# The first batch of a retention and mixer kernel: state sums, query scaling and constants in another order, and two weight loads moved

## The chip, the cores and the metric

The kernel runs on one core of a Trainium2 chip. The metric is the device time of one execution in microseconds (us). TensorE (PE) multiplies matrices, VectorE (DVE), ScalarE (ACT) and GpSimd (POOL) work elementwise, and SyncE (SP) and GpSimd start transfers between memory and the core.

## The reference

Inputs are q, k and v of 8 batches, 8 heads, 576 positions and 64 dimensions, and the weights U (576 x 32), V (32 x 576), w_ch1 (512 x 2048) and w_ch2 (2048 x 512), all in 32-bit floats.

```python
scores = (q @ k.transpose(0, 1, 3, 2)) / 8
gamma  = 1.0 - 2.0 ** (-5.0 - arange(8))            # one decay per head
rel    = pos[:, None] - pos[None, :]
x      = (scores * where(rel >= 0, gamma ** rel, 0)) @ v   # heads side by side: (8, 576, 512)
u      = x + (x.transpose(0, 2, 1) @ U @ V).transpose(0, 2, 1)
out    = u + maximum(u @ w_ch1, 0.0) @ w_ch2
```

The decay factors into one power of the query's position and one of the key's, so it is put into scaled queries or outputs, and into scaled keys.

## The kernel before

**Pairs and chunks.** Batches are worked in four pairs. The 1152 rows of a pair are nine chunks of 128; the middle one, J, holds the last 64 rows of one batch and the first 64 of the next. Batches after the first pair are cast, transposed by transfers and multiplied chunk by chunk in `section`.

**The first pair** is handled apart, since at the start everything waits for memory. Its rows are four units of 256 (u = 0 to 3 in the code, units one to four in the text), two for each batch, and the middle chunk J, in two halves. Lines are those of the kernel before:

- `early_consts` (L117) builds position and decay tables, masks and zeroed buffers on GpSimd, VectorE and ScalarE.
- `load_u` and `load_J` issue the loads of q, k and v on SyncE's queue. `load_w1` (L212) and `load_w2` issue the weights on GpSimd's queue, in pieces; `load_w1(f0, f1)` brings the columns of the groups f0 to f1 - 1.
- `scale_u` (L637) scales a unit's keys by `vscaleU` to bf16, `cast_u` (L630) casts queries and values, `cast_J` (L799) makes J's keys and queries; J's queries in the first half are scaled by `posJ` (L805).
- `T_u` (L646) transposes keys or queries on TensorE and copies them out. `SC_u` (L675) computes the scores of half of the heads, `mask_u` (L690) multiplies them with a triangle on VectorE (L692). `SC_off` (L719) computes the scores between the two rows of unit one and copies them to a buffer `off`. `RV_u` and `RV_off` multiply scores with values.
- `ST_u` (L760) sums key-value products of a unit into an accumulator, and `Sblk` (L770) copies that as a state block into `sblk`. `QS_u` (L744) adds queries times state to a unit's outputs. `XS_u` (L752) brings the outputs to the buffer `x`, on VectorE, times `qscale`.
- `T_J`, `SC_J`, `mask_J`, `RV_J`, `QS_J` and `XS_J` do the same for J.
- `warm(n)` (L205) issues n multiplications of the identity whose result is not used.
- `to_xT` transposes x, `MA` is the product with U, and then `first_stretch` (L1033) runs the products with w_ch1 (L515), group by group of 128 columns (f = 0 to 15), between the steps of units three and four. Its `y(n)` issues the next n groups. A piece of w1 has to be there when its first group comes.
- After unit four a one-element write by VectorE (L1089) releases the eight loads of w2.

**What sets the order.** The whole program is inside `tc.manual_schedule()`: every engine takes its instructions in the order in which the code issues them. Within one engine nothing overtakes. Buffers come from pools: PSUM has one buffer each of `psc` (`ps_sc`), `po` (`ps_o`) and `pss` (`ps_s`), and three of `big`. The next user of a buffer waits until its last reader is done. `SC_u(0, 1)` and then `SC_off(1)` both take `ps_o`, and `RV_u(0, ...)` takes `ps_sc` after `SC_u(1, 0)`.

## Time and profile before

| | us |
|---|---|
| median of 4 runs | 325.98 |
| lowest and highest of them | 325.44, 326.66 |
| the profiled execution | 327.3 |
| its span, from first to last instruction | 325.5 |
| TensorE busy | 311.1 |
| VectorE busy | 174.3 |
| ScalarE busy | 145.8 |
| GpSimd busy | 101.2 |

Times in the profile are counted from the start of the span. In the views of groups and of time, a line tells start or busy time, engine, code line, operation, what it writes and reads, and in brackets the idle time ahead of it with what ended that idle time. TensorE is the engine with the most work; idle time of the others costs nothing by itself. "Landing" of a transfer is the moment at which its last part is in place.

### The profile page before, as it was taken

The page shows a single profiled execution, that of the slowest core. Times are in us where ns is not written, and L with a number is a line of the kernel's source. Part 1 is how long each engine was busy: PE and PEld are TensorE (multiplying, and loading weights), DVE is VectorE, ACT ScalarE, POOL GpSimd, SP SyncE. Part 2 cuts the span into 40 slices and gives each one's busy share as a digit, 9 for nine tenths or more (in the row PEclk, how much of TensorE's full clock was granted, in tenths as well). Part 3 has the DMA queues.
Part 4 walks back from the last instruction along what each step waited for, and adds up shares of the span by engine and source line. Part 5 has one row for each costly group of instructions (what it writes and reads, how often), then busy time and mean ns, then how long its engine had stood idle before and what let it go on. Part 6 is the DMA issues. An engine that isn't in the chain of part 4 may idle for free.

```text
span 325.5 us, 9118 instructions
## 1 busy us (share of the span) xinstructions
PE 311.1 (96%) x3860; PEld 170.9 (53%) x3885; DVE 174.3 (54%) x342; ACT 145.8 (45%) x334; POOL 101.2 (31%) x172
## 2 busy tenths in 40 slices
PE   7899889999999999989999999999999999999996
PEld 3575545764444454446744454457644454467544
DVE  7866556229726578545844477556844475510012
ACT  6857547892020583048810484058800572047400
POOL 7796239223113722052221523152221500010000
PEclk9999999999999999999999999999999999999999
DMA  8999999999975989969996599859996450340022
GB/s 216 253 217 262 239 201 193 203 179 119 255 185 138 243 179 176 218 156 193 192 174 171 143 186 206 214 144 167 208 207 158 107 67 3 102 110 0 2 76 85
DMA packets 152904, 53.30 MB, mean 164 GB/s; under 512 B 132032, under 2 KB 150336, under 8 KB 152864
## 3 DMA queue, kind: packets, MB, share of 16 engines
q1 hardware_dynamic: 144512, 40.40, 67.8%
q0 software_dynamic: 8352, 12.32, 15.5%
q8 instruction: 30, 0.49, 0.6%
q14 instruction: 10, 0.08, 0.1%
HBM read 36.85 MB, written 9.44 MB: 142 GB/s over the span
## 4 chain that ended last, share of the span: by engine, by line
PE 72%; DMA 6%; ACT 3%; DVE 2%; issue 1%; DVEq 0%; SPq 0%
PE ps_y L549 34%; PE ps_y L515 30%; DMA qkT<-qk 5%; PE pp L296 2%; DVE u L464 2%; DMA uT<-u 1%; ACT y L520 1%; PE pp L316 1%; PE ps_y L560 1%; PE pp L328 1%; PE AB L358 1%; PE pa L431 1%; PE ph L458 1%; ACT s_sb L373 1%; ACT uT L489 0%
## 5 line engine op out<-in xcount | busy, mean ns | idle before, releaser
L515 PE MATMUL ps_y<-uT,w_sb 128*128 128x256 bf16 (+2 forms) x768 | 133.3, 326 | 2.6 <-DMA uT<-u 1.0
L520 ACT ACTIVATE y<-ps_y 128x384 bf16<-128x384 f32 (+2 forms) x192 | 89.6, 490 | 97.8 <-PE ps_y L515 97.0
L549 PE MATMUL ps_y<-w_sb,y 128*128 128x512 bf16 x535 | 123.8, 379 | 2.2 <-issue 1.1
L515 PEld LDWEIGHTS <-w_sb 128*128 128x128 bf16 x768 | 72.1, 98 | 50.6 <-issue 3.6
L549 PEld LDWEIGHTS <-y 128*128 128x128 bf16 x560 | 52.5, 98 | 61.2
L272 POOL TENSOR_TENSOR vt<-stage_t,vscale 64x256 bf16<-64x256 f32 (+1 forms) x81 | 50.4, 622 | 65.1 <-DMA stage_t<-in_v_dram 49.2
L538 DVE TENSOR_TENSOR o_sb<-ps_y,u 128x512 f32<-128x512 f32 (+2 forms) x38 | 25.2, 664 | 81.3 <-PE ps_y L549 79.0
L541 POOL DMA_DIRECT2D out_dram<-o_sb x31 | 17.1, 553 | 104.1 <-DVE o_sb L538 100.3
L304 DVE TENSOR_TENSOR ret<-pp,triH 128x512 bf16<-128x512 f32 x27 | 18.7, 691 | 24.5 <-PE pp L328 17.9
L464 DVE TENSOR_TENSOR u<-ph,xt 128x768 bf16<-128x768 f32 (+2 forms) x24 | 21.8, 950 | 5.9 <-PE ph L458 4.2
L437 ACT ACTIVATE a_sb<-pa 128x128 bf16<-128x128 f32 x8 | 2.2, 277 | 43.9 <-PE pa L431 43.9
L338 DVE COPY q<-qkT 64x256 bf16<-64x256 bf16 x48 | 14.1, 293 | 14.1 <-DMA qkT<-qk 13.2
L344 DVE TENSOR_TENSOR xt<-pp,qscale 128x512 bf16<-128x512 f32 x27 | 18.6, 689 | 4.7 <-PE pp L328 4.2
L263 DVE CAST qk<-stage_t 64x256 bf16<-64x256 f32 x54 | 19.2, 356 | 1.3
L383 DVE TENSOR_TENSOR s_sb<-AB,Af 64x256 bf16<-64x256 f32 x42 | 17.7, 422 | 2.1 <-ACT s_sb L378 1.5
L264 ACT ACTIVATE qk<-stage_t 128x512 bf16<-128x512 f32 x27 | 16.8, 622 | 0.0
L635 POOL CAST qk<-stage_t 128x512 bf16<-128x512 f32 x16 | 10.2, 638 | 11.6 <-DMA stage_t<-in_q_dram 6.5
L376 ACT ACTIVATE Af<-AB 128x256 f32<-128x256 f32 x24 | 9.2, 385 | 8.2 <-PE AB L358 7.7
L692 DVE TENSOR_TENSOR ret<-psc,triU 128x1024 bf16<-128x1024 f32 x8 | 9.6, 1206 | 3.3 <-PE psc L684 3.3
L261 ACT ACTIVATE qk<-stage_t 128x256 bf16<-128x256 f32 x27 | 11.1, 410 | 0.0
L296 PEld LDWEIGHTS <-qkT 64*64 64x64 bf16 x432 | 5.6, 107 | 10.2 <-issue 7.8
L209 PE MATMUL pw<-ident 128*128 128x512 bf16 x26 | 8.0, 452 | 1.4 <-POOL ident masks.py:199 1.4
(134 smaller groups left out, 220.0 us busy)
## 6 DMA issues: line engine op xcount, KB each, us to landing
stage_t<-in_k_dram SPq DMA_DIRECT2D x32, 256.0 KB, 4.8
stage_t<-in_q_dram SPq DMA_DIRECT2D x32, 256.0 KB, 5.5
stage_t<-in_v_dram SPq DMA_DIRECT2D x32, 256.0 KB, 5.7
out_dram<-o_sb POOLq DMA_DIRECT2D x31, 256.0 KB, 3.2
w_sb<-in_moe_w_ch_dram POOLq DMA_DIRECT2D x14, 256.0 KB, 8.1
stage_t<-in_k_dram SPq DMA_DIRECT2D x8, 128.0 KB, 3.3
stage_t<-in_q_dram SPq DMA_DIRECT2D x8, 128.0 KB, 3.6
stage_t<-in_v_dram SPq DMA_DIRECT2D x8, 128.0 KB, 4.1
```

Of the source, the lines that this page charges most:

```text
L263: nc.vector.tensor_copy(out=o[to, hl], in_=f[fr, hl])
L264: nc.scalar.activation(out=c["qk"][:, 0, :], in_=c["f", 0].rearrange("p h d -> p (h d)"), func=AF.Copy)
L272: nc.gpsimd.tensor_tensor(out=o[to, hl], in0=f[fr, hl], in1=w[fr, hl, :, None].to_broadcast([n, NHP, D]), op=ALU.mult)
L304: nc.vector.tensor_tensor(out=ret.rearrange("p a b i -> p a (b i)").rearrange("p a (b i) -> p a b i", i=D), in0=pp[:, :, 0:NHP * D].rearra ...
L344: nc.vector.tensor_tensor(out=st["x", pr][:, i, :].rearrange("p (hp hl d) -> p hl hp d", hl=2, d=D), in0=pp[:, :, NHP * D:2 * NHP * D].rea ...
L383: nc.vector.tensor_tensor(out=S_[half(x), 1, :], in0=Bk[half(1 - x)], in1=Af[half(1 - x), now, :], op=ALU.add)
L464: nc.vector.tensor_tensor(out=st["u", par][:, i0 - base:i0 - base + n, w].rearrange("p s (c d) -> p c s d", c=2), in0=ph[k][:, :, 0:n, :], ...
L515: nc.tensor.matmul(ps[:, 0:n, :], w1_sb[:, cc, f * P:(f + 1) * P], st["uT", par][:, c0:c0 + n, cc, :], start=(cc == 0), stop=(cc == NCC - 1),)
L520: nc.scalar.activation(out=st["y1", par][:, f, c0 * P:(c0 + n) * P], in_=ps[:, 0:n, :].rearrange("p s t -> p (s t)"), func=AF.Relu)
L538: nc.vector.tensor_tensor(out=o_sb[:, 0:n], in0=ps[:, 0:n], in1=st["u", par][:, c, w], op=ALU.add)
L541: (nc.sync if last else nc.gpsimd).dma_start(out=out_flat[r0:r0 + P, w], in_=o_sb[:, 0:n])
L549: nc.tensor.matmul(ps, st["y1", par][:, f, c * P:(c + 1) * P], w2_sb[:, f, :], start=(f == 0), stop=(f == NF - 1),)
```

## The change

It is made in `early_consts` and `startup`, and in three helpers that they call:

- In `early_consts`, ScalarE computes an exponential of `posU` for unit one. The position table, `qscale` and `vscale` are made ahead of the triangle `triU`. The zeroing of `sblk` and of `off` on VectorE moves here from `startup`.
- Unit one's queries are multiplied with that table on GpSimd instead of being cast, and `XS_u(0)` becomes a copy on ScalarE instead of a product on VectorE.
- `cast_J(0)` takes GpSimd for the keys instead of ScalarE, keeps VectorE for the queries, and stands ahead of unit two's transposes instead of behind its first mask. The first piece of w1 is issued right after it.
- Three warm-up multiplications after `SC_off(1)` go. Both sums of unit one (`acc1`, `acc2`) and the first state block come in their place. `T_J(0)` comes before unit one's outputs, and the sums and state blocks of unit two before its outputs.
- The steps from `RV_u(1, 1)` to `XS_J(0)` are written ahead of the casts and loads of GpSimd, with which they share no engine's order.
- `load_w1(10, 14)` moves from ahead of the keys and queries of unit four to behind them.

```diff
@@ -150,27 +150,31 @@
             out=posU.rearrange("p u j h -> p (u j) h"),
             in0=lngt[:, 0:8, :], in1=posU.rearrange("p u j h -> p (u j) h"), op=ALU.mult)
         nc.scalar.activation(out=vscaleU, in_=posU, func=AF.Exp, bias=lnb, scale=-1.0)
+        nc.scalar.activation(
+            out=posU[:, 0], in_=posU[:, 0], func=AF.Exp, bias=0.0, scale=1.0)
         nc.vector.tensor_scalar(
             out=posJ, in0=posJ, scalar1=0.5, scalar2=None, op0=ALU.mult)
         nc.vector.tensor_tensor(out=posJ, in0=posJ, in1=lngt[:, 0:2, :], op=ALU.mult)
         nc.scalar.activation(out=vscaleJ, in_=posJ, func=AF.Exp, bias=lnb, scale=-1.0)
         nc.scalar.activation(out=posJ, in_=posJ, func=AF.Exp, bias=0.0, scale=1.0)
+        nc.vector.tensor_scalar_add(pos[:, J + 1:NI, :], pos[:, J + 1:NI, :], -float(S))
+        nc.vector.tensor_scalar_add(pos[HALF:P, J, :], pos[HALF:P, J, :], -float(S))
+        nc.vector.tensor_tensor(out=lngt, in0=lngt, in1=pos, op=ALU.mult)
+        nc.scalar.activation(out=qscale, in_=lngt, func=AF.Exp, bias=0.0, scale=1.0)
+        nc.scalar.activation(out=vscale, in_=lngt, func=AF.Exp, bias=lnb, scale=-1.0)
         nc.vector.tensor_scalar(
             out=triU[0:HALF], in0=iotaU[0:HALF], scalar1=0.0, scalar2=None, op0=ALU.is_ge)
         nc.vector.tensor_scalar(
             out=triU[HALF:P], in0=iotaU[HALF:P], scalar1=-float(P), scalar2=None,
             op0=ALU.is_ge)
-        nc.vector.tensor_scalar_add(pos[:, J + 1:NI, :], pos[:, J + 1:NI, :], -float(S))
-        nc.vector.tensor_scalar_add(pos[HALF:P, J, :], pos[HALF:P, J, :], -float(S))
-        nc.vector.tensor_tensor(out=lngt, in0=lngt, in1=pos, op=ALU.mult)
-        nc.scalar.activation(out=qscale, in_=lngt, func=AF.Exp, bias=0.0, scale=1.0)
-        nc.scalar.activation(out=vscale, in_=lngt, func=AF.Exp, bias=lnb, scale=-1.0)
-        nc.vector.tensor_copy(out=triH[0:HALF], in_=tri[0:HALF, 0:HALF])
-        nc.vector.tensor_copy(out=triH[HALF:P], in_=tri[HALF:P, HALF:P])
+        nc.vector.memset(sblk, 0.0)
+        nc.vector.memset(un[0]["off"][HI], 0.0)
         nc.vector.memset(U_E[:, J, :], 0.0)
         nc.vector.memset(U_O[0:HALF, 0, :], 0.0)
         nc.vector.memset(V4[:, 0:HALF], 0.0)
         nc.vector.memset(V4[:, HALF + S:], 0.0)
+        nc.vector.tensor_copy(out=triH[0:HALF], in_=tri[0:HALF, 0:HALF])
+        nc.vector.tensor_copy(out=triH[HALF:P], in_=tri[HALF:P, HALF:P])
         nc.vector.tensor_copy(out=swap[:, 0:HALF], in_=ident[:, HALF:P])
         nc.vector.tensor_copy(out=swap[:, HALF:P], in_=ident[:, 0:HALF])
 
@@ -634,11 +638,11 @@
         else:
             eng.tensor_copy(out=o, in_=f)
 
-    def scale_u(u, hh, eng):
-        o, f = unit_views(u, 1, hh)
+    def scale_u(u, hh, eng, j=1):
+        o, f = unit_views(u, j, hh)
         eng.tensor_tensor(
             out=o, in0=f,
-            in1=vscaleU[:, u, :, 4 * hh:4 * hh + 4].rearrange("p j h -> p h j")[
+            in1=(posU, vscaleU)[j][:, u, :, 4 * hh:4 * hh + 4].rearrange("p j h -> p h j")[
                 :, :, :, None].to_broadcast([P, 4, 2, D]),
             op=ALU.mult,
         )
@@ -751,6 +755,11 @@
 
     def XS_u(u, c0=0, c1=2):
         i0, n = unit_i0(u) + c0, c1 - c0
+        if u == 0:
+
+            nc.scalar.activation(
+                out=st["x", 0][:, 0:2, :], in_=un[0]["po"], func=AF.Copy)
+            return
         nc.vector.tensor_tensor(
             out=st["x", 0][:, i0:i0 + n, :].rearrange("p s (h d) -> p s h d", d=D),
             in0=un[u]["po"][:, c0:c1, :].rearrange("p s (h d) -> p s h d", d=D),
@@ -904,7 +913,10 @@
         for hh in range(2):
             scale_u(u, hh, nc.gpsimd)
         for hh in range(2):
-            cast_u(u, 0, hh, nc.gpsimd)
+            if u == 0:
+                scale_u(u, hh, nc.gpsimd, 0)
+            else:
+                cast_u(u, 0, hh, nc.gpsimd)
 
     def startup():
         load_u(0, (1, 0))
@@ -921,7 +933,6 @@
         warm(10)
         cast_unit(0)
         T_u(0, 1, nc.vector)
-        nc.vector.memset(un[0]["off"][HI], 0.0)
         zero_J(1, nc.vector)
         load_J(1, (1, 0, 2))
         load_u(2, (1, 0, 2))
@@ -935,8 +946,9 @@
         cast_unit(1)
         cast_u(0, 2, 0, nc.gpsimd)
         cast_u(0, 2, 1, nc.gpsimd)
+        cast_J(0, nc.gpsimd, nc.vector)
+        load_w1(0, 2)
         cast_u(1, 2, 0, nc.gpsimd)
-        load_w1(0, 2)
         cast_u(1, 2, 1, nc.gpsimd)
         T_u(1, 1, nc.scalar)
         SC_u(0, 1, ps_o, "po")
@@ -944,32 +956,38 @@
         SC_off(0, ps_sc, "psc")
         warm(3)
         T_u(1, 0)
-        nc.vector.memset(sblk, 0.0)
         SC_off(1, ps_o, "po")
-        warm(3)
+        acc1 = pss_tile()
+        acc2 = ps_big.tile([P, NHP, P], FP32, tag="big", name="pss2")
+        ST_u(0, ALL, acc1, True)
+        Sblk(acc1, 1)
+        ST_u(0, ALL, acc2, True)
         SC_u(1, 0, ps_sc, "psc")
         mask_u(1, 0)
-        cast_J(0, nc.scalar, nc.vector)
         SC_u(1, 1, ps_o, "po")
         mask_u(1, 1)
-
-        acc1 = pss_tile()
-        ST_u(0, ALL, acc1, True)
-        Sblk(acc1, 1)
+        T_J(0)
         RV_u(0, 0)
         RV_u(0, 1)
         RV_off()
         XS_u(0)
-        T_J(0)
-        acc2 = ps_big.tile([P, NHP, P], FP32, tag="big", name="pss2")
-        ST_u(0, ALL, acc2, True)
+        SC_J(0)
+        mask_J(0)
         prep_vJ(0)
         cast_urows()
-        RV_u(1, 0)
-        SC_J(0)
-        mask_J(0)
         ST_u(1, LO, acc1, False)
         Sblk(acc1, 2)
+        ST_u(1, ALL, acc2, False)
+        Sblk(acc2, 3)
+        RV_u(1, 0)
+        RV_u(1, 1)
+        QS_u(1, 0, 1)
+        XS_u(1, 0, 1)
+        QS_u(1, 1, 2)
+        XS_u(1, 1, 2)
+        RV_J(0)
+        QS_J(3)
+        XS_J(0)
         cast_J(1, nc.gpsimd, nc.gpsimd)
         load_w1(2, 4)
         prep_vJ(1)
@@ -982,23 +1000,13 @@
         load_w1(8, 10)
         for hh in range(2):
             cast_u(2, 2, hh, nc.gpsimd)
-        load_w1(10, 14)
         scale_u(3, 0, nc.gpsimd)
         for hh in range(2):
             cast_u(3, 0, hh, nc.gpsimd)
+        load_w1(10, 14)
         load_w1(14, 16)
         for hh in range(2):
             cast_u(3, 2, hh, nc.gpsimd)
-        RV_u(1, 1)
-        QS_u(1, 0, 1)
-        XS_u(1, 0, 1)
-        ST_u(1, ALL, acc2, False)
-        Sblk(acc2, 3)
-        QS_u(1, 1, 2)
-        XS_u(1, 1, 2)
-        RV_J(0)
-        QS_J(3)
-        XS_J(0)
 
         xT = [ps_big.tile([P, dm], FP32, tag="big", name="xT") for _ in range(3)]
         xT.append(ps_sc.tile([P, dm], FP32, tag="psc", name="xT"))
```

## The prediction

> **What bounds the kernel now.** I read the page's busy table first, then its 40 slices, then TensorE's timeline with the waits in brackets.

> ```profile
> PE 311.1 (96%) x3860; PEld 170.9 (53%) x3885; DVE 174.3 (54%) x342; ACT 145.8 (45%) x334; POOL 101.2 (31%) x172
> ...
> PEclk9999999999999999999999999999999999999999
> ```

> TensorE is busy 311.1 of 325.5 us at full clock. The change touches only the first 48 us, so its worth is what it adds to or takes from TensorE's work and idle time there, as far as later waits do not swallow it. The table of stages gives TensorE 7.84, 8.94, 9.12, 9.09 and 9.13 us busy in the first five tens, 19.47 of 20 from 80 to 100 and 170.19 of 175 after 150: idle time worth having is all early. In TensorE's timeline of 0 to 48 us these lines matter:

> ```profile
> 11.65 0.41 PE L726 MATMUL psx<-qkT 64*64 64x128 bf16 x8 [0.35 <-DVE ret L692]
> 11.99 0.82 PE L209 MATMUL pw<-ident 128*128 128x512 bf16 x3
> 12.65 0.61 PE L655 MATMUL pst<-ident,qk 128*128 128x128 bf16 x8
> 13.19 0.41 PE L726 MATMUL psx<-qkT 64*64 64x128 bf16 x8
> 13.54 0.82 PE L209 MATMUL pw<-ident 128*128 128x512 bf16 x3
> 14.29 0.86 PE L684 MATMUL psc<-qkT 64*64 64x128 bf16 x32
> ...
> 16.21 0.64 PE L711 MATMUL po<-qk,ret 64*128 64x64 bf16 x32 [0.52 <-DVE ret L692]
> ...
> 38.42 0.51 PE L655 MATMUL pst<-ident,qk 128*128 128x128 bf16 x6 [0.91 <-POOL qk L635]
> ...
> 41.91 0.38 PE L763 MATMUL pss<-qk 64*128 64x128 bf16 x4 [0.42 <-POOL qk L635]
> 42.23 0.42 PE L684 MATMUL psc<-qkT 64*64 64x128 bf16 x16
> 42.58 1.04 PE L515 MATMUL ps_y<-uT,w_sb 128*128 128x512 bf16 x4
> ```

> Start, duration, group, then idle time and its releaser. Up to 24 us TensorE idles in short pieces; the second batch of cross scores (L726, 13.19) waits for nothing. At 38.42 and 41.91 it waits for GpSimd's casts of unit four's queries and values, which come from memory. At 42.58 stands the eleventh group of the first matrix (f = 10).

> VectorE's timeline, SyncE's, and the transfer view cut to the moment of one issue:

> ```profile
> 10.44 2.29 DVE L692 TENSOR_TENSOR ret<-psc,triU 128x1024 bf16<-128x1024 f32 x2
> 13.30 0.73 DVE L665 COPY qkT<-pst 128x512 bf16<-128x512 bf16 x1 [0.57 <-PE pst L655]
> ...
> 16.08 0.85 DVE L805 TENSOR_TENSOR qk<-stage_t,posJ 128x512 bf16<-128x512 f32 x1
> ```
> ```profile
> 9.04 0.82 SPq L796 DMA_DIRECT2D stage_t<-in_q_dram  x1
> ```
> ```profile
> stage_t<-in_q_dram SPq DMA_DIRECT2D x1, 128.0 KB, 5.0
> ```

> The queries of the middle chunk J are issued at 9.04 and land 5.0 us later, at **14.0**. Before, VectorE scales them (L805) at 16.08, long after, and both of unit one's masks are over at 12.73.

> [...] GpSimd's in-order queue sits 1.42 us before the value cast at 14.90, and the w1 issue behind it comes only at 15.46. [...] This trace has no gap over 1.4 us and a granted clock of 1.0 throughout[...]. [...] with w1 in flight from 36.8 to 40.5 us the DMA share is 1.19, and SyncE's last loads take 7 to 12 us instead of 5.

> **The change part by part.**

> *Queries of unit one scaled instead of cast.* Two GpSimd casts (0.63 and 0.61, L635) become two products with a scale, at 1.06 as L639. The first starts at 6.34 as before; the second ends at 8.46 instead of 7.78. TensorE's transposes at 7.84 start 0.65 later. ScalarE's added exponential (0.22, like L157) lies before 3.4 us, covered by the wait for the first keys. Unit one's output copy leaves VectorE (1.21, L754) for ScalarE (1.02, like L730).

> *Constants reordered.* VectorE clears sblk and the cross buffer (0.91 each) ahead of the key copy L669, which then ends near 9.4 instead of 7.60. The second small product of L199 needs its PSUM buffer and TensorE gets there near 9.2: +0.2. The earlier qscale and vscale have no early reader: zero.

> *J's query cast moved ahead of the mask of unit one's second half.* The instruction order of the changed kernel shows VectorE: first mask, J's scaling (waiting for that transfer), second mask. Nothing before it in SyncE's queue moves, so I keep 14.0. Scaling 14.05 to 14.90, mask 14.90 to 16.10 (1.15 to 1.21, L692). Behind it stand VectorE's copy of unit two's queries and the second cross scores, which need that PSUM buffer. They start at **16.15 instead of 13.19**. TensorE is ready near 14.1, so it idles 2 us; the +0.65 and +0.2 above vanish inside this.

> *From there to the transposition of x.* Before, 13.19 to 21.83, 8.64 us. After, by starts: cross scores 0.35 (16.50); both sums of unit one 1.12 in place of three warm-ups of 0.75 (17.62); scores of unit two 0.79 (18.41); J's transposes 0.44 (18.85). The outputs of unit one take the buffer that the first mask of unit two frees: scores out at 18.05, 0.15 to VectorE, 1.19 of mask, 19.40, so 0.55 idle, as 0.52 before. Outputs 1.06 (20.46), J's scores 0.2, the sums of unit two 1.05 (21.7), its outputs 0.75 (22.45). The second state product starts 1.18 after the first, as before (19.73, 20.91), since the copy-out of the first row of the same tile lies between; the sum that stood in this gap has moved away, so it is idle now. 23.63, then 0.92 as before: **24.55, +2.7**. The gains (0.75 of warm-ups, waits of 0.17 and 0.34) are spent on this gap and the sums' new place. ScalarE's outputs of unit one (20.6 to 21.7) push the later state copies to 23.2, before their reader at 24.2: free.

> *GpSimd's part of that.* J's key cast moves there (0.60, from ScalarE's 0.62) into a 1.42 wait and w1's first piece is issued 1.35 earlier; nothing on TensorE reads it before 27: zero, or a few tenths late for unit two's values, which have 2 us of slack.

> *w1 pieces behind unit four's queries.* Before:

> ```profile
> 30.56 0.74 POOL L214 DMA_DIRECT2D w_sb<-in_moe_w_ch_dram  x1
> ...
> 37.75 0.61 POOL L635 CAST qk<-stage_t 128x512 bf16<-128x512 f32 x1 [2.14 <-DMA stage_t<-in_q_dram]
> 38.30 0.81 POOL L214 DMA_DIRECT2D w_sb<-in_moe_w_ch_dram  x1
> ```
> ```profile
> w_sb<-in_moe_w_ch_dram POOLq DMA_DIRECT2D x1, 512.0 KB, 9.9
> ```

> The piece for f = 10 to 13 is issued at 30.56 and lands at 40.5, 2.1 us early. Now it stands behind the query casts. The software queue moved 0.45 MB in 34 to 38 us, much of it this piece, so the last queries may land up to 1 us sooner; the issue then falls at 37.5 to 38.4. A 256 KB piece takes 5.5 to 6.0 us from issue with nothing ahead of it (the ones at 15.46 and 38.30), a further 256 KB 1.8 to 3 more: landing 44.5 to 47; I take **45.2**, towards the early end[...]. TensorE comes to f = 10 at 42.58 + 2.7, less the two waits at 38.42 and 41.91 that a late TensorE no longer meets (0.91 + 0.42): 44.0. Stall 1.2 (0 to 3). The next piece has 4 us more.

> *Sum.* +2.7 − 1.3 + 1.2 = +2.6. The matrix loads of w2 start as much later; between 50 and 80 us the waits for transposes, uT and y come to 2 us, but casts, w2 and transposes hang on the same shifted TensorE, so I let them swallow 0.2 only. **+2.4 us.** Against the profiled execution (327.3, of which 325.5 span) that is 329.7; that execution lies 1.3 above the median 325.98, so the forecast is **328.4**.

> **The rivals.** *w1 in time.* If the piece lands by 44.0 only +1.4 is left, less 0.2: 327.2. For it: freed transfer time. Against: 5.5 us even for half its size.

> *Swallowed.* If in addition the waits of 50 to 80 us swallow half a microsecond or more, 326.5, no measurable change. For it: transposes that take 6.5 and 5.1 us there. Against: their casts shift with TensorE.

> *Faster.* J's queries land by 11.4, before the first mask's end less the scaling; then the second mask is not held and TensorE reaches unit four with no delay, where queries a microsecond sooner take away the waits of 0.91 and 0.42: about −1.0, 325.0. It decides at a landing of 11.4 against 14.0 seen; 2.6 us is far.

> *Worse.* The 2 us gap beside the shorter ones halves the granted clock for a window, or w1 lands at 47: +4.5, 330.5.

> The change's scheduling does reach the instruction streams, so "it does nothing" is no case.

> **How the numbers follow.** Forecast 0.52, w1 in time 0.26, swallowed 0.09, faster 0.05, worse 0.08. 0.3% of this kernel is 1.0 us, about what a measurement tells from no change; "faster" takes its case, "same" the swallowed one with the low edge of w1 in time (0.10), "slower" the rest (0.85). The likeliest case alone spans 327.5 to 330; the range reaches down through w1 in time and up to the worse case: 326.6 to 330.6.

> **What would show it.** In the changed profile: VectorE idle about 1.7 us before J's scaling, released by the transfer of q; the second cross scores of TensorE near 16.1, after about 2 us idle on VectorE's mask; the transposition of x near 24.5; no wait on GpSimd for unit four's queries; at f = 10 a wait for w1. I am wrong if J's scaling does not wait, if x is transposed before 23, or if w1's late piece is never waited for.

## The result, and the profile after

The changed kernel takes 327.95 us (median of 38 executions, 326.37 to 330.5) against 325.97 (57 executions, 324.56 to 330.63): **ratio 1.0064, 95% interval 1.005 to 1.0078**, 2.0 us slower. (That of the two medians is 1.0061; ratios below are the recorded ones too.) The forecast was 328.4, 2.4 us slower than 325.98. The profiled execution takes 327.94 us, of which 326.2 are its span.

The page of the changed kernel, busy times and granted clock:

```profile
PE 311.4 (95%) x3857; PEld 171.2 (52%) x3882; DVE 174.3 (53%) x341; ACT 146.3 (45%) x335; POOL 102.6 (31%) x173
...
PEclk9799999999999999999999999999999999999999
```

TensorE is busy as long as before. New is the second digit of the clock: 7 where before every slice had 9. The profiled execution is thus one of those in which the clock dropped; none of the changed kernel at full clock was profiled. TensorE's timeline of the changed kernel:

```profile
8.24 0.28 PE L659 MATMUL pst<-ident,qk 128*128 128x128 bf16 x2 [0.72 <-POOL qk L643]
9.25 0.51 PE L659 MATMUL pst<-ident,qk 128*128 128x128 bf16 x6 [0.73 <-POOL qk L643]
9.69 0.38 PE L203 MATMUL pv<-V_b,fan 32*128 32x512 bf16 x1
10.98 0.18 PE L203 MATMUL pv<-V_b,fan 32*128 32x64 bf16 x1 [0.90 <-DVE qkT L673]
11.10 2.29 PE L213 MATMUL pw<-ident 128*128 128x512 bf16 x5
13.32 0.64 PE L688 MATMUL psc<-qkT 64*64 64x128 bf16 x16
...
17.03 0.41 PE L730 MATMUL psx<-qkT 64*64 64x128 bf16 x8
...
24.24 0.40 PE L750 MATMUL po<-sblk,qkT 128*128 128x128 bf16 x4 [0.79 <-DVE xt L763]
...
25.16 0.62 PE L1017 MATMUL xT<-ident,xt 128*128 128x128 bf16 x8
...
40.57 0.61 PE L659 MATMUL pst<-ident,qk 128*128 128x128 bf16 x8
...
43.69 0.62 PE L772 MATMUL pss<-qk 64*128 64x128 bf16 x8
...
44.59 1.04 PE L519 MATMUL ps_y<-uT,w_sb 128*128 128x512 bf16 x4
```

The same steps in the kernel before:

```profile
7.84 0.51 PE L655 MATMUL pst<-ident,qk 128*128 128x128 bf16 x6 [0.24 <-POOL qk L635]
...
8.63 1.25 PE L209 MATMUL pw<-ident 128*128 128x512 bf16 x5
9.82 0.42 PE L684 MATMUL psc<-qkT 64*64 64x128 bf16 x16
...
21.83 0.62 PE L1009 MATMUL xT<-ident,xt 128*128 128x128 bf16 x8
```

Three readings. The first scores of unit one (L688) start at 13.32; before they started at 9.82. So 3.5 us are lost already here, ahead of the step where the prediction put its loss. From here on the gap hardly grows: x is transposed (L1017) at 25.16 instead of 21.83, +3.3. Then the waits for unit four's queries and values are gone (40.57 and 43.69 have no bracket, where 0.91 and 0.42 stood), and the eleventh group (44.59, f = 10) comes 2.0 us later than its 42.58, with no wait for w1. The end is 2.0 us later by the medians too. The two profiled spans differ by 0.7 only. In part that is because the waits of TensorE after 48 us hold one in the kernel before that the changed one lacks:

```profile
PE ps_y L515 <- DMA uT<-u: 1.0, 1, 1.0
```

The 3.5 us can be split in that view. The second transposes of unit one's queries begin at 9.25 instead of 7.84: +1.41. VectorE's copy holds the second product of L203, so that the warm-ups of L213 begin at 11.10 instead of 8.63: +1.06 more. Five warm-ups take 2.22 us to the next group instead of 1.19: +1.03. VectorE's and GpSimd's timelines of the changed kernel tell where the first two come from:

```profile
6.41 0.91 DVE L171 MEMSET y<- 64x1024 uint32 x1 [0.27 <-issue]
...
7.57 0.64 DVE L176 COPY triH<-y 64x64 bf16<-64x64 bf16 x1
8.22 1.00 DVE L177 COPY triH<-y 64x64 bf16<-64x64 bf16 x1
9.24 1.00 DVE L178 COPY swap<-ident 128x64 bf16<-128x64 bf16 x1
10.16 0.17 DVE L179 COPY swap<-ident 128x64 bf16<-128x64 bf16 x1
10.25 0.68 DVE L673 COPY qkT<-pst 128x1024 bf16<-128x1024 bf16 x1
...
14.01 1.23 DVE L696 TENSOR_TENSOR ret<-psc,triU 128x1024 bf16<-128x1024 f32 x1 [1.47 <-PE psc L688]
15.15 0.68 DVE L814 TENSOR_TENSOR qk<-stage_t,posJ 128x512 bf16<-128x512 f32 x1
15.75 1.22 DVE L696 TENSOR_TENSOR ret<-psc,triU 128x1024 bf16<-128x1024 f32 x1
```
```profile
7.12 2.07 POOL L643 TENSOR_TENSOR qk<-stage_t,posU 128x512 bf16<-128x512 f32 x2 [1.25 <-DMA stage_t<-in_q_dram]
9.15 2.09 POOL L643 TENSOR_TENSOR qk<-stage_t,vscaleU 128x512 bf16<-128x512 f32 x2
```

VectorE's copies in the kernel before:

```profile
4.84 1.03 DVE L168 COPY triH<-y 64x64 bf16<-64x64 bf16 x1
5.89 0.18 DVE L169 COPY triH<-y 64x64 bf16<-64x64 bf16 x1
...
6.32 0.18 DVE L174 COPY swap<-ident 128x64 bf16<-128x64 bf16 x1
6.42 0.59 DVE L175 COPY swap<-ident 128x64 bf16<-128x64 bf16 x1
6.92 0.68 DVE L669 COPY qkT<-pst 128x1024 bf16<-128x1024 bf16 x1
```

The query products start at 7.12, 0.78 after the cast of before (6.34), since the transfer came later in this execution, and take 2.07 instead of two casts. The clearings (that of L171, named `y`, is of the cross buffer `off`) end at 7.32, and now the small copies of the constants fall beside four GpSimd products in a row, which end about 8.16, 9.19, 10.2 and 11.2. The copies L176 to L178 end at 8.21, 9.22 and 10.24, each as a product ends; L179, of the same shape as L178, takes 0.17. Behind them the key copy (L673) ends at 10.93; before (L669) it ended at 7.60. In the kernel before two of the copies are long in the same way: L168 (1.03) ends at 5.87 and L175 (0.59) at 7.01, beside a product and a cast of GpSimd that end at 5.84 and 6.97; L169 and L174 take 0.18. What makes them end together was not shown.

J's scaling (L814) does not wait: no bracket. J's queries had landed at 14.53, and the mask ahead of it ended later because the first scores were late. TensorE hardly waits behind it either: its transposes end at 16.90, the second mask at 16.97, and the second cross scores start at 17.03.

### The profile page after: what moved, and what is told of

Read it like the earlier page. It is cut to its first block, busy times and chain, and to the rows that moved or that the text cites. A ratio compares the mean times of both kernels' runs of the same rounds, so it can differ in the third digit from the quotient of the medians.

```text
span 326.2 us, 9115 instructions
## 1 busy us (share of the span) xinstructions
PE 311.4 (95%) x3857; PEld 171.2 (52%) x3882; DVE 174.3 (53%) x341; ACT 146.3 (45%) x335; POOL 102.6 (31%) x173
## 4 chain that ended last, share of the span: by engine, by line
PE 74%; ACT 4%; DMA 3%; DVE 2%; issue 1%; DVEq 0%
PE ps_y L553 34%; PE ps_y L519 32%; PE pp L300 2%; DVE u L468 2%; DMA qkT<-qk 1%; ACT y L524 1%; DMA uT<-u 1%; PE pp L320 1%; PE pp L332 1%; PE ps_y L564 1%; PE AB L362 1%; PE pa L435 1%; PE ph L462 1%; ACT s_sb L377 1%; ACT qk L268 0%
## 5 line engine op out<-in xcount | busy, mean ns | idle before, releaser
L639 POOL CAST qk<-stage_t 128x512 bf16<-128x512 f32 x14 | 9.1, 671 | 4.1 <-DMA stage_t<-in_q_dram 3.6
L213 PE MATMUL pw<-ident 128*128 128x512 bf16 x23 | 8.1, 507 | 1.4 <-POOL ident masks.py:199 1.4
## 6 DMA issues: line engine op xcount, KB each, us to landing
stage_t<-in_k_dram SPq DMA_DIRECT2D x8, 128.0 KB, 3.7
stage_t<-in_q_dram SPq DMA_DIRECT2D x8, 128.0 KB, 4.0
stage_t<-in_v_dram SPq DMA_DIRECT2D x8, 128.0 KB, 3.8
```

## The experiments

Every ratio is to the kernel before, run in turn on the same chip. "Full" counts executions whose mean granted clock over the span is 0.998 or more, "low" the others; the median of each is shown as a ratio to the median of before. One window of 3.41 us at half clock brings that mean to 0.995 (as in u_zero's profile), and most low executions are at 0.994 or 0.995. The kernel before had medians of 325.97, 326.56, 326.59 and 327.26 in four series (after; u_zero to b_w1; u_scale to b_split in the table; the last four), so small differences between ratios of different series are less sure than the intervals say.

| kernel | ratio [95%] | full: number, ratio | low: number, ratio |
|---|---|---|---|
| after | 1.0064 [1.005, 1.0078] | 20, 1.0034 | 18, 1.0089 |
| u_zero | 1.0038 [1.0021, 1.0055] | 6, 1.0007 | 13, 1.0041 |
| u_jq | 1.0022 [1.0003, 1.004] | 11, 0.9984 | 11, 1.0047 |
| u_zero_jq | 0.9998 [0.9979, 1.0018] | 17, 0.9979 | 5, 1.0067 |
| b_w1 | 1.0017 [0.9995, 1.0039] | 12, 0.9978 | 10, 1.0055 |
| u_scale | 1.0058 [1.0039, 1.0078] | 9, 1.0043 | 13, 1.0072 |
| clk | 1.0041 [1.002, 1.0062] | 9, 1.0036 | 4, 1.0076 |
| u_all | 0.9983 [0.9967, 0.9999] | 21, 0.9984 | 1, 1.0145 |
| b_split | 1.0009 [0.998, 1.0038] | 12, 1.0007 | 2, 1.0099 |
| u_scale_warm | 1.0025 [1.001, 1.0041] | 22, 1.0015 | 0 |
| u_w1 | 1.0004 [0.9988, 1.002] | 14, 0.9998 | 8, 1.0013 |
| best1 | 0.9969 [0.9949, 0.9989] | 19, 0.9957 | 3, 1.0097 |
| best2 | 0.9986 [0.9967, 1.0004] | 22, 0.9970 | 0 |

The kernel before is at full clock in nearly all of its executions (5 low ones in 204). The changed kernel is not: its low executions have a median of 328.86, its full ones 327.09. The profiled executions of after, u_zero, u_jq, u_zero_jq, u_scale, clk and u_w1 are all low ones; what those kernels do at full clock is known by their times alone.

**The theories.** *Hold*: the loss is the mask held behind J's scaling. *Start*: it is the clearings and the products ahead of the first scores. *w1*: it is the late piece. *Clock*: it is the granted clock. The expectations below write theory P for *Hold*, as in the prediction, and theory H (head start) for *Start* together with *Clock*.

**u_zero: the two clearings back where they were.**

```diff
@@ early_consts @@
-        nc.vector.memset(sblk, 0.0)
-        nc.vector.memset(un[0]["off"][HI], 0.0)
@@ startup @@
         T_u(0, 1, nc.vector)
+        nc.vector.memset(un[0]["off"][HI], 0.0)
...
         T_u(1, 0)
+        nc.vector.memset(sblk, 0.0)
         SC_off(1, ps_o, "po")
```

> The changed kernel with the two clearings on VectorE (sblk and the cross buffer) back at their old places. Theory H (head start: the clearings and the slower query scaling make the first scores so late that J's queries have already landed; TensorE's idle pieces beside that let the granted clock drop in some executions): the second product of L203 no longer waits on VectorE (0.9 us in the changed profile), the first scores start near 11.2 to 11.5 instead of 13.3, the clock stays at 1.0, but now J's scaling waits for its transfer (landing 14.3 to 14.6) and the second cross scores start near 16.5 instead of 17.0. Time 327.3, about 0.6 under the changed kernel. Theory P (as in the prediction: J's scaling alone sets the second cross scores): they stay at 17.0 and the time at 328.0, within 0.3.

Measured 1.0038. In its TensorE timeline the first scores come at 10.82, 2.5 us sooner than in the changed kernel. Then the predicted hold appears, on VectorE and behind it on TensorE:

```profile
14.42 0.69 DVE L812 TENSOR_TENSOR qk<-stage_t,posJ 128x512 bf16<-128x512 f32 x1 [1.91 <-DMA stage_t<-in_q_dram]
```
```profile
16.30 0.41 PE L728 MATMUL psx<-qkT 64*64 64x128 bf16 x8 [2.12 <-DVE ret L694]
16.64 1.88 PE L770 MATMUL pss<-qk 128*128 128x128 bf16 x16
```

VectorE idles 1.91 us for J's queries, TensorE 2.12 us for the mask behind. The second cross scores start at 16.30; the prediction said 16.15. After that gap the sums of L770 take 1.88 us, at a granted clock of 0.50 from 16.69 to 20.10; they take 1.07 in the changed kernel. So in this execution the 2.5 us won are down to 0.7 at the cross scores, and gone where x is transposed, at 25.48 against 25.16. The time is the one that theory H forecast (a ratio of 1.004), but not its clock of 1.0: 13 of 19 executions are low, and in the profiled one the drop follows the new gap. VectorE's key copy is early again:

```profile
7.23 0.68 DVE L671 COPY qkT<-pst 128x1024 bf16<-128x1024 bf16 x1
```

**u_jq: J's scaling alone behind the copy of unit two's queries.** `cast_J` is split for that: the first call casts the keys, the second scales the queries.

```diff
-        cast_J(0, nc.gpsimd, nc.vector)
+        cast_J(0, nc.gpsimd, None)
...
         T_u(1, 0)
+        cast_J(0, None, nc.vector)
         SC_off(1, ps_o, "po")
```

> The changed kernel with only VectorE's scaling of J's queries moved from ahead of the second mask to behind the copy of unit two's queries; GpSimd keeps the key cast and the early first w1 piece. Theory P: the second cross scores lose the whole wait and the time falls by 2 us, to 326.0. Theory H: the first scores are late anyway, so only the 0.7 us of the scaling itself goes: second cross scores near 16.4, time 327.4, and the clock still drops in some executions.

Measured 1.0022, between the two theories (1.0001 and 1.0044). The interval ends below that of the changed kernel, so the place of J's scaling is a real part of the loss, by the ratios 1.4 us. That counts the wait for the transfer and the 0.6 us of the scaling itself ahead of the second mask. Its profiled execution does not show the gain, because the start is worse in it: VectorE's copies take 0.91, 1.00, 1.00 and 0.64, and TensorE waits 2.38 us for the key copy.

```profile
11.71 0.21 PE L203 MATMUL pv<-V_b,fan 32*128 32x64 bf16 x1 [2.38 <-DVE qkT L673]
11.85 2.31 PE L213 MATMUL pw<-ident 128*128 128x512 bf16 x5
```

**u_zero_jq: both edits.**

```diff
@@ early_consts @@
-        nc.vector.memset(sblk, 0.0)
-        nc.vector.memset(un[0]["off"][HI], 0.0)
@@ startup @@
+        nc.vector.memset(un[0]["off"][HI], 0.0)
...
-        cast_J(0, nc.gpsimd, nc.vector)
+        cast_J(0, nc.gpsimd, None)
...
         T_u(1, 0)
+        cast_J(0, None, nc.vector)
+        nc.vector.memset(sblk, 0.0)
         SC_off(1, ps_o, "po")
```

> Both of the former together. Theory H: the two hide each other, so together they give more than the sum: second cross scores near 14.2 (2.8 us earlier than the changed kernel), x transposed near 22.5. How much of it reaches the end is set by the late w1 piece, which landed at 43.2 in the changed profile: the eleventh group then waits there for 1 us or more; time 326.6. Theory P: the same as the kernel with J's scaling moved alone, 326.0, and no wait for w1.

Measured 0.9998: with both undone nothing is left of the loss, as theory P forecast. The trace is that of theory H. In the profiled execution, one of the 5 low ones, the second cross scores start at 13.42 and x is transposed at 22.09. But here TensorE is early enough to meet the late w1 piece:

```profile
44.11 1.76 PE L517 MATMUL ps_y<-uT,w_sb 128*128 128x512 bf16 x4 [2.54 <-DMA w_sb<-in_moe_w_ch_dram]
```

It waits 2.54 us, and then four multiplications take 1.76 instead of 1.04 us, at half clock (0.50 from 44.27 to 47.69).

**b_w1: the late w1 piece alone, on the kernel before.**

```diff
-        load_w1(10, 14)
         scale_u(3, 0, nc.gpsimd)
         for hh in range(2):
             cast_u(3, 0, hh, nc.gpsimd)
+        load_w1(10, 14)
```

> The kernel before with only the w1 piece for f = 10 to 13 moved behind unit four's queries. By the prediction's rule (landing 45.2 or later): TensorE loses its waits of 0.9 and 0.4 us on unit four and gains one of 3.9 at f = 10, time 328.6. By the changed kernel's trace (landing 43.2): the wait at f = 10 is 1.9, net 0.6, time 326.6. Rival: the freed transfers bring the queries forward and the piece is in time, then 325.0.

Measured 1.0017, not told apart from no change, and near the 1.0019 that the changed kernel's trace gave. The profile has both of the predicted effects: no wait for unit four's casts, and the wait at f = 10:

```profile
43.60 1.04 PE L515 MATMUL ps_y<-uT,w_sb 128*128 128x512 bf16 x4 [1.74 <-DMA w_sb<-in_moe_w_ch_dram]
```

The one element of VectorE that releases w2 comes at 47.84 instead of 46.81, so up to there the late piece costs more than it gains in this execution, which is at full clock. Its span is 324.8 us all the same, 0.7 less than that of before: the later wait of 1.0 for uT is missing here too. The 12 executions at full clock have a median of 0.9978; they may be the ones in which the wait was short enough to leave the clock alone (1.74 us in the profiled one), so this figure alone shows no gain.

**u_w1: only the late w1 piece back, in the changed kernel.** (The edit of b_w1, the other way.)

```diff
+        load_w1(10, 14)
         scale_u(3, 0, nc.gpsimd)
         for hh in range(2):
             cast_u(3, 0, hh, nc.gpsimd)
-        load_w1(10, 14)
```

> The changed kernel with only the late w1 piece back ahead of unit four's keys. The changed profile shows TensorE coming to unit four's queries and to f = 10 later than either transfer's landing, so with or without the move there is nothing to wait for: ratio as of the changed kernel, 1.0064 within 0.2%. By the prediction's sum (a wait of 1.2 us at f = 10) it falls by 1.2 us, to 1.0027.

A miss: 1.0004, below the interval of the changed kernel and below the 1.0027 of the prediction's sum too. Yet its profiled execution has x at 25.47 and w2 released at 49.13, as late as the changed kernel (48.82). The late piece landed at 43.16 in the changed kernel's profile, 1.4 us ahead of its group, and between 42.2 and 44.1 in the runs that have it late; in executions at full clock TensorE may come sooner and wait, but none of those was profiled. The kernel before was slower than usual in this series (327.26), and the changed kernel was not run beside it; the medians of the two, 327.28 and 327.95, lie 0.7 us apart. What the late piece costs in the changed kernel stays open, between nothing (its profile) and all of it (this ratio).

**u_scale: unit one's queries cast again, outputs by VectorE.**

```diff
-            if u == 0:
-                scale_u(u, hh, nc.gpsimd, 0)
-            else:
-                cast_u(u, 0, hh, nc.gpsimd)
+            cast_u(u, 0, hh, nc.gpsimd)
```

(and in `XS_u` the branch with ScalarE's copy left out.)

> The changed kernel with unit one's queries cast again (and its outputs multiplied on VectorE). Theory H: two GpSimd products of 1.06 become casts of 0.62, and VectorE's copies of constants, which took 0.6 to 1.0 us beside GpSimd's products, mostly return to 0.2; the first scores start near 11 instead of 13.3 although both clearings stay, and J's scaling now waits for its transfer: second cross scores near 16.3 after about 2 us of idle TensorE, with a clock drop behind it in some executions. Time 327.6, as with the clearings undone. Rival: the scaling costs only its own 0.8 us of GpSimd, so the first scores start near 12.6 and the clock drops there as before; 328.0.

Measured 1.0058, no different from the changed kernel. The constants' copies are back to 0.39, 0.18, 0.18 and 0.60 although the clearings still stand ahead of them; beside the GpSimd products of the changed kernel they took 0.64, 1.00, 1.00 and 0.17. The key copy behind them is early:

```profile
7.93 0.68 DVE L673 COPY qkT<-pst 128x1024 bf16<-128x1024 bf16 x1
```

So neither part alone makes it late. It ends at 7.60 in the kernel before, at 7.91 and 7.78 with the products alone (u_zero, u_zero_jq), at 8.61 and 8.30 with the clearings alone (u_scale, u_scale_warm), and at 10.93, 11.66, 11.48 and 11.80 with both (after, u_jq, clk, u_w1). The first scores come at 10.01. Of the 3.3 us won, the hold leaves 0.95 at the second cross scores, and at half clock behind it (0.50 from 16.37 to 19.78) nothing is left where x is transposed (25.27):

```profile
16.08 0.41 PE L730 MATMUL psx<-qkT 64*64 64x128 bf16 x8 [2.71 <-DVE ret L696]
16.43 1.89 PE L767 MATMUL pss<-qk 128*128 128x128 bf16 x16
```

**clk: more warm-ups where the start of the changed kernel idles.**

```diff
-        warm(5)
+        warm(8)
         nc.scalar.activation(out=V_b, in_=V_f, func=AF.Copy)
         T_u(0, 0, nc.scalar)
-        make_v()
         warm(5)
+        make_v()
```

> The changed kernel with eight warm-up products instead of five ahead of the transposes of unit one's queries, and the next five ahead of the V products instead of behind them: the same waits, but TensorE has something to do in them. Theory H: the granted clock stays 1.0 until 16 us, the first scores start near 12.2, second cross scores near 16.5; the median falls by 0.9, to the 327.1 that the changed kernel's executions at full clock show. Rival: the clock is a bystander; the waits are what counts, and three more products make it no faster: 328.0 or more.

A miss: 1.0041, not told apart from the changed kernel, with 9 of 13 executions at full clock against 20 of 38. The drop moved from 11.2 to 13.8 us. The window ahead of it (10.40 to 13.82) is busy for 1.70 of 3.42 us, with waits of 0.86 and 1.27 us where the warm-ups do not stand, the second of them reaching past its end.

**u_scale_warm: twelve warm-ups in the gap of u_scale.**

```diff
         T_u(1, 0)
+        warm(12)
         SC_off(1, ps_o, "po")
```

> The kernel with the query cast back, in which TensorE idled 2.7 us before the second cross scores, plus twelve warm-up products (12 x 0.22 = 2.6 us) in that gap: the wait on J's queries stays, only the idling goes. If the idle gap lets the clock drop: the clock stays 1.0 up to 24 us, the sums behind the gap take 1.1 instead of 1.9 us and the scores 0.64 instead of 1.07, x is transposed near 24.0 instead of 25.3, and the median falls by 0.6 to 0.9 to a ratio near 1.0035, with hardly an execution below full clock. Rival: the drop has nothing to do with the gap; the ratio stays at 1.006 and half of the executions stay below full clock.

Measured 1.0025 against 1.0058 for the same kernel without them (medians of 327.74 and 328.36 us), 22 of 22 executions at full clock against 9 of 22. x is transposed at 24.46 instead of 25.27. The stretches of TensorE's clock, first of u_scale, then of u_scale_warm (stretch, length, busy us of TensorE, its weight loads, VectorE, ScalarE and GpSimd, granted clock, DMA share, GB/s):

```profile
12.96:16.37 3.41, 0.70 (x16) 0.58 (x13) 2.17 (x3) 0.96 (x2) 3.17 (x5) 1.00 1.04 222
16.37:19.78 3.41, 3.41 (x59) 2.99 (x55) 1.14 (x2) 1.72 (x3) 2.23 (x6) 0.50 1.18 230
19.78:23.20 3.42, 3.31 (x110) 2.86 (x109) 3.25 (x5) 1.89 (x5) 3.38 (x5) 1.00 1.09 292
```
```profile
12.96:16.37 3.41, 3.26 (x23) 1.68 (x23) 1.93 (x3) 1.18 (x2) 3.05 (x5) 1.00 0.91 190
16.37:19.78 3.41, 2.85 (x90) 2.48 (x91) 2.19 (x3) 2.54 (x5) 2.32 (x5) 1.00 1.16 213
```

Without the warm-ups TensorE is busy 0.70 of 3.41 us and the next stretch runs at 0.50; with them it is busy 3.26 and the clock stays. Work whose result nobody reads made the kernel faster. And in the changed kernel:

```profile
7.75:11.16 3.41, 1.29 (x11) 0.63 (x12) 3.33 (x6) 2.05 (x3) 3.41 (x4) 1.00 1.13 286
11.16:14.58 3.42, 3.42 (x29) 1.58 (x29) 1.84 (x4) 0.50 (x2) 2.85 (x6) 0.50 1.11 259
```

TensorE is busy 1.29 of 3.41 us, with gaps of 0.7 to 0.9. Then come 3.42 us at half clock.

**u_all: clearings, J's scaling, query casts and w1 all back.** What remains of the change is TensorE's new order, the earlier `qscale` and `vscale`, J's keys on GpSimd and the earlier first w1 piece.

It has the edits of u_zero_jq and u_scale, and this one:

```diff
+        load_w1(10, 14)
         scale_u(3, 0, nc.gpsimd)
...
-        load_w1(10, 14)
         load_w1(14, 16)
```

> The changed kernel with the clearings, J's query scaling, the query cast and the late w1 piece all back as before: left are TensorE's new order (sums instead of three warm-ups, outputs after the sums), the earlier qscale and vscale, and J's keys on GpSimd with the first w1 piece earlier. Theory H: the new order is worth nothing by itself; second cross scores near 13.2, x transposed at 21.9 against 21.83, release of w2 at 46.8; time 326.0, within 0.3% of the kernel before. Rival: the new order itself loses, by the wider gap between the two state products, then x is transposed after 22.5 and the time is over 326.7.

Measured 0.9983, 21 of 22 executions at full clock. What remains does no harm and may help, although x is transposed at 22.20, 0.37 later than before; the loss was in the parts taken back.

**b_split: before, with the w1 piece cut in two, one half late.**

```diff
-        load_w1(10, 14)
+        load_w1(10, 12)
         scale_u(3, 0, nc.gpsimd)
         for hh in range(2):
             cast_u(3, 0, hh, nc.gpsimd)
+        load_w1(12, 14)
```

> The kernel before with the 512 KB w1 piece cut in two: f = 10 and 11 stay at the old place, f = 12 and 13 go behind unit four's queries. If the late landing was what spoilt the move of the whole piece: half of the freed transfers bring the queries forward, TensorE's waits of 0.9 and 0.4 us on unit four fall to 0.4 or less in all, no wait for w1, time 325.1. Rival: half of the traffic is not enough to bring the queries forward, or the extra issue of 0.8 us holds the value casts: 326.0.

A miss: 1.0009, near the rival's 1.0001. The early gain is there (w2 released at 45.88 instead of 46.81) and is given back at the chunk transposes, by TensorE's waits after 48 us:

```profile
PE pp L296 <- DMA qkT<-qk: 2.7, 3, 1.2
```

Before, this wait was 0.5 us in all.

**best1 and best2: u_all with two gaps of its own closed, and that with the cut piece.**

```diff
@@ best1, against u_all @@
         mask_u(0, 1)
+        nc.vector.memset(sblk, 0.0)
         SC_off(0, ps_sc, "psc")
...
         cast_J(0, None, nc.vector)
-        nc.vector.memset(sblk, 0.0)
...
         XS_u(1, 0, 1)
-        QS_u(1, 1, 2)
-        XS_u(1, 1, 2)
         RV_J(0)
         QS_J(3)
+        QS_u(1, 1, 2)
+        XS_u(1, 1, 2)
         XS_J(0)
@@ best2, against best1 @@
-        load_w1(10, 14)
+        load_w1(10, 12)
...
+        load_w1(12, 14)
         load_w1(14, 16)
```

> The kernel with the four parts undone (0.9983 of the kernel before), and two moves more: sblk is cleared between VectorE's second mask and its copy of unit two's queries, so that it no longer stands before the mask on which unit one's outputs wait (1.27 us of idle TensorE, 0.7 less), and J's outputs go between the two state products of unit two (0.79 us of idle, 0.6 less). x is transposed near 20.9 instead of 22.2. If unit four's queries set the pace from there, their wait grows from 0.44 to 1.7 us and nothing of it reaches the end: 0.998. If not: 0.994.

> The former with the 512 KB piece of w1 cut in two, the second half behind unit four's queries. If unit four's queries set the pace, they come 0.4 us or so sooner and release of w2 falls from near 46.1 to 45.6: 0.9965. Rival: what is gained there is given back in the later waits for chunk transposes, as the cut kernel without the other changes showed (2.7 us of such waits instead of 0.5): 0.998.

best1 is at 0.9969 [0.9949, 0.9989], faster than the kernel before beside it (327.26) and than the changed one: x is transposed at 20.60 instead of 21.83. Its median of 325.88 is hardly below the lowest of the four medians of before, 325.97. best2 (0.9986) releases w2 earlier still, at 45.39 instead of 46.71, and ends no earlier: its waits for chunk transposes are 2.7 us, those of best1 1.9. As in b_split, what is won ahead of w2 is lost again where the chunks wait for their transposes.

## Why the prediction was right, and where it was not

**The number and the sign** held: +2.0 measured, +2.4 forecast. The sum behind it held in part only, and that the number came out is in part luck. Up to f = 10 it was 2.7 − 1.3 + 1.2 = 2.6; the profile has 3.3 − 1.3 + 0 = 2.0. The 3.3 came by another path than the forecast 2.7, and the stall that did not come more than makes up for it.

**The hold is real, and worth less than its term.** VectorE stands 1.91 and 2.50 us before J's scaling in u_zero and u_scale, and the second cross scores come at 16.30 and 16.08 there against the 16.15 forecast. Undoing it alone takes 0.42% off (u_jq), about 1.4 us of the 2.0, the scaling's own time included. But the changed kernel's own profile does not show it: of the three signs of being wrong that the prediction set, two came true in that execution, J's scaling that does not wait and the w1 piece that is never waited for. Whether the hold shows in the changed kernel at full clock, where the start may come sooner, no profile tells.

**The failed step: "the +0.65 and +0.2 above vanish inside this".** The start was 3.5 us late, not 0.85, and so it hid the hold rather than the other way. What was mis-sized is the wait of the second product of L203 (0.2 forecast; 0.90 in the changed kernel, 2.38 in u_jq), because the key copy ahead of it was forecast to end near 9.4 and ends at 10.93 to 11.80. I moved the clearings and lengthened GpSimd's work and costed each alone; that the small VectorE copies would then lie beside GpSimd's products and take up to 1.00 us each, I did not see. u_scale and u_zero show it: without the products or without the clearings the key copy is done by 8.61. The clock drop adds 1.03, and the late landing of this execution 0.78. Without that landing the start is no sooner: in u_jq and u_w1 the query products start at 6.37 and 6.52, and the key copy ends later still. So two delays stand one behind the other. In the profiled executions undoing the clearings moves the second cross scores by 0.7 us, undoing both by 3.6. The ratios don't show that: 0.26% and 0.42% alone, 0.66% together, each to about 0.2%, is what two gains that simply add up would give too. With the w1 piece of u_w1 (0.60%) the single gains would come to twice the loss of 0.64%, so they are not to be read as shares of it.

**The clock was the underrated rival.** I gave half clock for a window to the worse case; its 0.08 was my estimate. The trace before, in which TensorE's longest gap is 1.36 us, has no such drop; in the changed kernel's profile the window ahead of the drop is busy 0.38 of the time. The drop came in 18 of 38 executions, whose median lies 1.77 us above that of the others: 18/38 x 1.77 = 0.84 of the 2.0 us. The other 1.1 us (327.09 against 325.97) is what the executions at full clock lose. Not all of the 1.77 need be the clock. A window of 3.41 us at half clock (0.50) can take at most 1.7, by an estimate from these two numbers, but in u_zero_jq the low executions lie 2.87 above the others: an execution that waits longer may have both the idle time and the drop. u_scale_warm shows what brings the drop: filling the idle stretch, from 0.70 to 3.26 us busy of 3.41, takes it away (22 of 22 executions at full clock instead of 9), which is worth 0.6 us by the medians there.

**From the cross scores to x** I had 8.40 us; the profile has 8.13. The new gap between the state products is there, 0.79. **The waits at unit four** are swallowed as forecast, 0.91 and 0.42.

**The stall at f = 10** was forecast at 1.2 and is 0 in the changed kernel's profile. Issue at 37.24 was a little early, and the 512 KB took 5.9 us to land: I had put a 256 KB piece at 5.5 to 6 and added up to 3 for the second half. TensorE came at 44.6 instead of 44.0. The case "w1 in time" (0.26) is what that execution shows. The stall itself is no fiction: b_w1 and u_zero_jq, where TensorE is ready 2.7 and 3.0 us sooner, wait 1.74 and 2.54 us for the same piece. Its share in the changed kernel stays open, as said with u_w1.

## What to carry to other kernels

When an instruction that waits for a transfer is moved up an in-order queue, compare its landing with the moment its new place is reached; but then look for the delay that stands second, since the one can hide the other, as in the profiles here. Cost small VectorE copies by what GpSimd runs beside them in the new order, not by their old durations (one shape took 0.17 or 1.00 us here). Gaps of TensorE that each look too short to matter, here of 0.7 to 0.9 us, together left it busy for 1.29 of 3.41 us, and the clock was 0.50 after it; cheap filler work there is worth a trial (0.6 us in u_scale_warm). A time won early counts only if the next transfer-bound stage can use it: in b_split w2 was released 0.93 us sooner, and the waits for chunk transposes grew from 0.5 to 2.7 us.

## What the runs showed of the hardware

```profile
10.40:13.81 3.41, 1.70 (x42) 1.01 (x41) 3.24 (x6) 2.07 (x4) 2.66 (x5) 1.00 1.26 265
```
```profile
65.29:68.70 3.41, 1.90 (x37) 1.27 (x35) 1.48 (x5) 2.63 (x8) 1.10 (x2) 1.00 1.00 188
```

In clk the longest gap within the window is 0.86 us and the clock drops after it; in best2 it is 1.51 us and the clock stays. So here the drop goes with the busy share, not with the length of one gap. The longest gap ahead of a drop is 2.71 us, in u_scale. The first border on record lies between 4.3 and 7.3 us from the start of the span and differs by execution. By an estimate from the changed kernel's profile, a window of 3.41 us is busy half or less if it starts between 6.9 and 8.2 us, and if borders fall evenly, one falls there in 0.37 of the executions. Counting windows that are busy 0.55 or less, it would be 0.74. The 18 low ones of 38 lie between; how long TensorE idles in the others was not profiled.
